# Windowed attention and an MLP mixer: 32-bit transposes of q and k pairs, natural order for the first two groups, and v loaded on 128 partitions

## Chip, cores and metric

The kernel runs on one core of one Trainium2 chip. The metric is the time of one execution on the device, in microseconds (us). A run that is more than 1.5% above the fastest of its kernel counts as slow and is left out of the ratios. Engine names: PE is TensorE (PEld its weight loads), DVE is VectorE, ACT is ScalarE, POOL is GpSimd, SP is SyncE. The program fixes the order of each engine's instructions, and in the traces one that waits holds up those behind it: after the change k of group 1 is cast at 41.85 us, right behind v's cast, and at 25.08 us when it is put ahead of it (run 1). In the DMA views q1 is SP's queue, q10 ACT's and q0 (software) POOL's.

## The reference

Four batches, eight heads, 768 positions, 64 columns per head; a window of 128 plus four sink positions. The attention output is the input x (768 x 512 per batch) of an MLP mixer.

```python
scores = scale * (q @ k.T);  keep = (pos_k < 4) | ((rel >= 0) & (rel < 128))
x = softmax(where(keep, scores, -1e9)) @ v            # (B, S, H*D)
u = x + (relu(x.T @ w_tok1) @ w_tok2).T               # token mixing, w_tok1 768x256, w_tok2 256x768
out = u + relu(u @ w_ch1) @ w_ch2                     # channel mixing, w_ch1 512x1536, w_ch2 1536x512
```

## The kernel before

The kernel handles eight groups of four heads, two groups per batch. Per group, q, k and v arrive as fp32, are cast to bf16, q and k are transposed in 32x32 blocks on DVE, scores run on 32-row tiles of PE, ACT takes the exps, DVE or POOL multiplies by masks, PE multiplies by v, and DVE normalises into x_b. When both groups of a batch are there, token mixing, u, the transposed u and then the channel mixer (ps_v with w_ch1, ps_w with w_ch2) follow.

The author's own planner fixes the order of the instructions of each engine. It simulates durations and landing times and picks, again and again, the operation that could start first.

```python
def order_of(ops, slots):
    ...
        if o.land:                                   # a DMA: modelled landing time
            dma_free = max(dma_free, t + 1.2) + o.land
            o.end = dma_free + 0.9
```

A dependency in this list orders the plan. It becomes a wait on the chip only where one instruction really reads or overwrites what the other one writes.

```python
    def load_ops(g, deps, pri):                      # cut
        run = E if g < 2 else 1                      # 1 KB runs for groups 0 and 1, 256 B later
        ...
                    e = "ACT" if g == 0 and w == "k" else "SP"
                        head_load(nc.scalar if e == "ACT" else nc.sync, G, w, heads(src, g), h, lo, hi, run)
    ...
        def turn(w, hf, db, c):                      # two 16-bit transposes for each of q and k
                nc.vector.transpose(G.T[w][:, db, ds(hf * HS, S // n_half)],
                                    G.bf[w][:, hf].rearrange("p (r x j) -> p r x j", x=DB, j=Q)[:, :, db])
    ...
    def weight(key, dst, src, deps, pri=-40):
        def emit(e):
            nc.gpsimd.dma_start(out=dst, in_=src)    # casts fp32 to bf16 on the way
    v1st = groups[0].load["v"][3]                    # "after v of group 0": known to the planner only
    weight("tok1", w_tok1, ..., [v1st]); weight("tok2", w_tok2, ..., [v1st])
    c1w = [weight(("ch1", i), ..., [v1st], ...) for i in range(4)]
```

For groups 0 and 1, v also comes in 1 KB runs of four rows, so it has to be spread to its rows by small matmuls (ps_p).

The softmax here doesn't subtract the row's maximum and nothing guards it: scores larger than these inputs give would overflow.

Of the kernel before, what the change touches and what calls it, by code (L numbers as in the profile page):

```python
# [12 lines left out]
ALU = mybir.AluOpType  # L13

# [10 lines left out]
class Op:  # L25


    n = 0

    def __init__(self, name, engines, emit, deps=(), pri=0, rows=False, take=(), free=(), land=0.0, dear=None):  # L30
        self.name, self.engines, self.emit = name, engines, emit
        self.deps, self.pri, self.rows = [d for d in deps if d is not None], pri, rows
        self.take, self.free, self.land, self.dear = take, free, land, dear or {}
        self.far = 0.0
        self.begin = self.end = self.engine = None
        Op.n += 1
        self.seq = Op.n
# [11 lines left out]
def order_of(ops, slots):  # L49
# [3 lines left out]
    dma_free, rows = 1.9, False  # L53
    for o in reversed(sorted(ops, key=lambda o: o.seq)):
        for d in o.deps:
            d.far = max(d.far, o.far + min(o.engines.values()) + (0.2 if "PE" in d.engines else 0.07))
# [3 lines left out]
    def start(op, e):  # L60
# [3 lines left out]
        if op.take:  # L64
            for kind in {p.kind for p in op.take}:
                n = sum(p.kind == kind for p in op.take)
                t = max(t, sorted(banks[kind])[n - 1])
        if e == "PE" and op.rows != rows:
            t += 0.095
        return t  # L70

    while waiting:
# [16 lines left out]
        t, e, o = best  # L89
        o.begin, o.engine = t, e  # L90
# [3 lines left out]
        if o.land:  # L94
            dma_free = max(dma_free, t + 1.2) + o.land
            o.end = dma_free + 0.9
        else:
# [22 lines left out]
def kernel(  # L120
# [101 lines left out]

    def c_ident(e):
        make_identity(nc, ident)
# [7 lines left out]
    def c_mneg(e):  # L232
        z = mneg.rearrange("p m (x c e i) -> p (m x) c e i", c=2, e=E, i=Q)
        nc.gpsimd.affine_select(out=z[:, :, 0], in_=z[:, :, 0], compare_op=ALU.is_ge, fill=-30000.0, base=0,
                                pattern=[[0, 4], [1, E], [E, Q]], channel_multiplier=-1)
        nc.gpsimd.affine_select(out=z[:, :, 1], in_=z[:, :, 1], compare_op=ALU.is_ge, fill=-30000.0, base=-1,
                                pattern=[[0, 4], [-1, E], [-E, Q]], channel_multiplier=1)
# [57 lines left out]
    BW, BWV = 0.37, 0.17  # L295
# [4 lines left out]
    def head_load(eng, G, w, src, h, lo, hi, run):  # L300

        n = (hi - lo) // (Q * run)
        at = lo // (Q * run)
        eng.dma_start(  # L304
            out=G.raw[w][Q * h:Q * h + Q].rearrange("p (c x) -> p c x", x=run * D)[:, at:at + n],
            in_=src[h, lo:hi].rearrange("(c i e) d -> i c (e d)", i=Q, e=run))

    def load_ops(g, deps, pri):
# [3 lines left out]
        run = E if g < 2 else 1  # L312
        for w, src in (("q", q), ("k", k), ("v", v)):
            if w == "v" and g >= 2:
                def vv(e):
                    t = G.raw["v"] = raw_tile("v")
                    nc.sync.dma_start(out=t.rearrange("p (h t d) -> p (h t) d", h=GH, t=NT),
                                      in_=heads(v, g).rearrange("h (t p) d -> p (h t) d", p=P))
                G.load["v"] = [op(f"Lv{g}", ("SP", 0.87), vv, deps, pri + 1, land=mb / BWV)]
                continue  # L320
            parts = [(0, HS), (HS, S)] if g == 0 and w != "v" else [(0, S)]
            G.load[w] = []
            for lo, hi in parts:
                for h in range(GH):
                    e = "ACT" if g == 0 and w == "k" else "SP"

                    def emit(_, w=w, src=src, h=h, lo=lo, hi=hi, e=e):
                        if w not in G.raw:
                            G.raw[w] = raw_tile(w)
                        head_load(nc.scalar if e == "ACT" else nc.sync, G, w, heads(src, g), h, lo, hi, run)  # L330
                    G.load[w].append(op(f"L{w}{g}.{lo}{h}", (e, 0.47), emit, deps,
                                        pri + (w == "v") * (50.5 if g == 0 else 1) + (lo > 0), land=mb / 4 * (hi - lo) / S / (BW if g < 2 else BWV)))


    def attention(g, xb, base):
# [3 lines left out]
        perm, pem = g < 2, g < 1  # L339
        early = base - 30 if perm else base  # L340
# [5 lines left out]
        def cast(w, hf):  # L346
# [5 lines left out]
            if perm:  # L352
# [3 lines left out]
            deps = G.load[w][4 * hf:4 * hf + 4] if first else G.load[w]  # L356
            return op(f"C{w}{g}.{hf}", eng, emit, deps + (prev.dt[w] if prev else []), early, dear={"DVE": 0.5 * g})

        def turn(w, hf, db, c):
            def emit(e):  # L360
                if w not in G.T:
                    G.T[w] = att.tile([P, DB, S], BF16, name=w + "T")
                nc.vector.transpose(G.T[w][:, db, ds(hf * HS, S // n_half)],  # L363
                                    G.bf[w][:, hf].rearrange("p (r x j) -> p r x j", x=DB, j=Q)[:, :, db])
            old = (prev.sc + [prev.sk]) if prev else []
            return op(f"T{w}{g}.{hf}{db}", ("DVE", dve(nc_ / 2) - 0.06), emit, [c] + old, early)

        casts, dts = {}, {"q": [], "k": []}
        for hf in range(n_half):
            for w in "qk":  # L370
                casts[w, hf] = cast(w, hf)
            for w in "qk":
                dts[w].append([turn(w, hf, db, casts[w, hf]) for db in range(DB)])
# [5 lines left out]
        if perm:  # L379
            def castv(e):  # L380
                G.vb = bfp.tile([P, NT, E, D], BF16, name="vb")
                copy_on[e](G.vb.rearrange("p t e d -> p (t e d)"), G.raw["v"])
            N = GH * S * D // P
            cv = op(f"Cv{g}", {"POOL": 1.02e-3 * N, "DVE": dve(N, 2)}, castv, G.load["v"], -5,
                    dear={"DVE": 0.3})
            ph = [Psum("mx", 1) for _ in range(GH)]

            G.cv = []
            for h in range(GH):
                def spread(e, h=h):  # L390
                    r = ds(Q * h, Q)
                    open_psum(ph[h], [P, NT, D], FP32, "ps_p")
                    for x in range(E):
                        nc.tensor.matmul(ph[h].tile[ds(Q * x, Q)], ident[r, r], G.vb[r, :, x],
                                         start=True, stop=True, tile_position=(Q * h, Q * x))
                sp = op(f"VP{g}.{h}", ("PE", 0.18), spread, [cv, c_ident_op], -5, rows=2, take=[ph[h]])

                def take(e, h=h):
                    copy_on[e](G.va[:, h, :, 0:D], ph[h].tile)
                G.cv.append(op(f"VE{g}.{h}", {"ACT": act(NT * D), "DVE": dve(NT * D)}, take, [sp, c_va_op] + old,  # L400
                               -5, free=[ph[h]]))
            G.cast.append(cv)
        else:
            def castv(e):
                copy_on[e](G.va[:, :, :, 0:D], G.raw["v"].rearrange("p (h t d) -> p h t d", h=GH, t=NT))
            G.cv = [op(f"Cv{g}", {"POOL": 1.55}, castv, G.load["v"] + [c_va_op] + old, base + 2)]
            G.cast += G.cv

        def sinkkeys(e):
            nc.vector.tensor_tensor(  # L410
                out=kz[g % 2][:, :, 0:4 * GH].rearrange("p x (h s) -> p x h s", h=GH),
                in0=(G.T["k"][:, :, 0:P:Q] if perm else G.T["k"][:, :, 0:4]).rearrange(
                    "p x (o s) -> p x o s", o=1).to_broadcast([P, DB, GH, 4]),
# [6 lines left out]
        def scores(u, hs, ps):  # L420
# [3 lines left out]
            def emit(e):  # L424
# [3 lines left out]
                if pem:  # L428
                    for h in hs:
                        nc.tensor.matmul(bank[h][:, 0:n], ident_e, mneg[:, min(u, 1), 0:n],  # L430
                                         start=True, stop=False, skip_group_check=True)
                at = 0
                for kt, w in nk:
                    for db in range(DB):
                        for h in hs:
                            r = ds(Q * h, Q)
                            nc.tensor.matmul(bank[h][:, at:at + w], G.T["k"][r, db, ts(kt, P)],  # L437
                                             G.T["q"][r, db, ds(kt * P, w)],
# [6 lines left out]
            if pem:  # L445
                dur += 0.19 + len(hs) * (n / 2400 + 0.003)
                deps += [c_mneg_op]
# [19 lines left out]
        def masks(u, ex):  # L467
# [21 lines left out]
            for x in xs:  # L489
                for c in range(2 if 2 * u + x < NT - 1 else 1):  # L490
                    r.append(op(f"MK{g}.{u}{x}{c}", {"DVE": dve(512, 2)} if perm else {"POOL": 0.72, "DVE": dve(512, 2) + 0.1}, lambda e, x=x, c=c: block(e, x, c),
# [21 lines left out]
        def sink_scores(e):  # L513
            ps = open_psum(pk_ps, [P, 512], FP32, "ps_k")
            for db in range(DB):
                nc.tensor.matmul(ps, kz[g % 2][:, db], G.T["q"][:, db, 2 * P:S], start=db == 0, stop=db == DB - 1)
# [53 lines left out]
    def mixer(b, base, mbase):  # L570
# [23 lines left out]
        M.t2, M.u, M.ut, M.ute = [], [], [], []  # L594
        M.ut_sb, M.u_sb = None, None
        M.uT = [None, None]
        cols = [(a, a * W, W) for a in range(GB)] if b == 0 else [(None, 0, DM)]
        M.ute = [[] for _ in range(NT)]
        for a, lo, n in cols:
            h1s = M.h1 if a is None else M.h1[NTOK * a:NTOK * a + NTOK]  # L600
            for st in range(NT):
                p, p2 = Psum("mx", 1), Psum("mx", 1)

                def tok2(e, st=st, p=p, lo=lo, n=n):
                    ps = open_psum(p, [P, n], FP32, "ps_u")
                    for tt in range(NTOK):
                        nc.tensor.matmul(ps, w_tok2[:, tt, ts(st, P)], M.h1t[:, tt, ds(lo, n)],  # L607
                                         start=(tt == 0), stop=(tt == NTOK - 1))

                def uadd(e, st=st, p=p, lo=lo, n=n):  # L610
# [201 lines left out]
```

## Time and profile before

| | before |
|---|---|
| time | 225.53 us (median of 2 runs, 225.16 to 225.91) |
| busy: PE, DVE, ACT, POOL | 206.2, 127.4, 107.5, 70.2 us |
| v of group 1 has landed (its cast starts) | 26.56 us |
| first channel-mixer matmul | 47.69 us |
| from there to the last PE work | 173.0 us |

These are the row of the page with busy times, and the row of the clock that TensorE was granted, in 40 slices of 5.6 us (9 is full speed).

```profile
PE 206.2 (92%) x1760; PEld 115.9 (52%) x1780; DVE 127.4 (57%) x271; ACT 107.5 (48%) x187; POOL 70.2 (31%) x89
...
PEclk9955569999999999999999999999999999999999
```

The next view is the table of windows: start:end, length, then busy time and instructions of each engine, the granted clock, the share of the DMA engines and GB/s.

```profile
core 0: us, PE busy (x) PEld busy (x) DVE busy (x) ACT busy (x) POOL busy (x), PEclk, DMA share, GB/s
0.00:12.00 12.00, 6.74 (x27) 2.42 (x28) 8.33 (x18) 3.51 (x6) 7.35 (x22) 0.98 0.97 174
12.00:32.00 20.00, 15.98 (x139) 6.70 (x139) 12.16 (x23) 9.99 (x16) 9.03 (x12) 0.50 1.24 199
...
48.00:221.00 173.00, 169.97 (x1433) 96.88 (x1449) 93.16 (x187) 86.31 (x150) 52.33 (x54) 1.00 0.65 116
```

From 48 us on PE is busy for 169.97 of 173 us, so that stretch is bound by PE. Everything before it is a start-up of 48 us that waits for data. The chain of waits (start, duration, what), read around that start-up, shows for what:

```profile
10.88 7.93 DMA raw_k<-in_k_dram
18.82 7.61 DMA raw_v<-in_v_dram
26.56 1.36 DVE vb L199
27.96 1.43 PE ps_p L394 x12
...
47.69 2.38 PE ps_v L645 x14
```

The DMA view from 20 to 26 us (queue, packets, MB, share of 16 engines' time) has one line of data, SP's queue; no weight packet moved before about 26 us, when v of group 1 was in:

```profile
q1 hardware_dynamic: 1907, 1.21, 117.9%
```

Of the groups of instructions these lines concern the change: transposes and masks (count, busy us, mean ns).

```profile
L212 POOL TENSOR_SCALAR_AFFINE_SELECT pT<-pT 128x512 bf16<-128x512 bf16 x21 | 15.9, 765 | 35.4 <-ACT pT L456 14.9
...
L363 DVE STREAM_TRANSPOSE kT<-kb 128x768 bf16<-128x768 bf16 (+1 forms) x18 | 15.0, 863 | 11.4 <-POOL kb L200 10.7
```

### The profile page before, as it was taken

The numbers are of one execution on the slowest core, as the hardware profiler recorded it, in microseconds if no ns is written. First come the engines' busy times: TensorE is split into PE (matmuls) and PEld (weight loads), VectorE is DVE, ScalarE is ACT, GpSimd is POOL, SyncE is SP. The second block draws the span as 40 slices with busy tenths as digits, with TensorE's granted clock in tenths as the row PEclk, the third lists the DMA queues.
The fourth block names the chain that finished last, engine by engine and source line by source line (L and its number), as shares of the span: only waits on it lengthen the run. The fifth ranks groups of instructions, "written<-read, shape, count | busy, mean of one in ns | idle before, by whom it ended". The sixth has DMA issues, their size and how long they took to land.

```text
span 223.9 us, 4412 instructions
## 1 busy us (share of the span) xinstructions
PE 206.2 (92%) x1760; PEld 115.9 (52%) x1780; DVE 127.4 (57%) x271; ACT 107.5 (48%) x187; POOL 70.2 (31%) x89
## 2 busy tenths in 40 slices
PE   7298497999999999999999899999999999999994
PEld 2023165766557546555656554456755544655543
DVE  7665498780378558958948984698672113001122
ACT  0466346357574481489583470288653400763300
POOL 6616800200467265418639232174200000000000
PEclk9955569999999999999999999999999999999999
DMA  7999999999999199899999499500001112101122
GB/s 149 200 202 207 186 194 192 193 197 199 180 164 209 39 198 171 210 195 169 190 167 202 114 166 189 194 3 3 0 1 40 56 47 94 50 0 47 47 97 94
DMA packets 70212, 29.40 MB, mean 131 GB/s; under 512 B 57776, under 2 KB 67248, under 8 KB 70192
## 3 DMA queue, kind: packets, MB, share of 16 engines
q1 hardware_dynamic: 63984, 24.39, 61.8%
q0 software_dynamic: 5312, 3.95, 11.6%
q10 hardware_dynamic: 896, 0.79, 1.8%
q8 instruction: 14, 0.23, 0.5%
q14 instruction: 6, 0.05, 0.1%
HBM read 26.77 MB, written 6.29 MB: 148 GB/s over the span
## 4 chain that ended last, share of the span: by engine, by line
PE 75%; DMA 10%; DVE 7%; ACT 4%; SPq 1%; issue 1%; DVEq 0%
PE ps_w L667 27%; PE ps_v L645 26%; DMA raw_k<-in_k_dram 7%; PE ps_u L607 5%; PE ps_h L583 5%; PE ps_s L437 4%; DMA raw_v<-in_v_dram 3%; PE ps_ut L618 3%; DVE pT L477 2%; PE ps_o L538 2%; PE ps_o L543 2%; PE ps_o L535 2%; DVE x_b L559 2%; ACT pT L456 1%; SPq L304 1%
## 5 line engine op out<-in xcount | busy, mean ns | idle before, releaser
L645 PE MATMUL ps_v<-uT,w_ch 128*128 128x384 bf16 x384 | 69.0, 326 | 0.8 <-DVE x_b L559 0.6
L667 PE MATMUL ps_w<-w_ch,v 128*128 128x512 bf16 (+1 forms) x288 | 65.2, 370 | 0.8 <-issue 0.2
L205 ACT ACTIVATE v<-ps_v 128x384 bf16<-128x384 f32 x86 | 42.0, 493 | 43.2 <-PE ps_v L645 32.1
L645 PEld LDWEIGHTS <-w_ch 128*128 128x128 bf16 x384 | 35.8, 98 | 24.8 <-DVE x_b L559 1.7
L677 DVE TENSOR_TENSOR o<-ps_w,u_sb 128x512 f32<-128x512 f32 (+1 forms) x25 | 16.7, 666 | 52.0 <-PE ps_w L667 52.0
L667 PEld LDWEIGHTS <-v 128*128 128x128 bf16 x300 | 28.6, 98 | 30.2 <-issue 0.4
L456 ACT ACTIVATE pT<-ps_s 128x1024 bf16<-128x1024 f32 (+1 forms) x36 | 32.4, 950 | 20.2 <-PE ps_s L437 17.7
L212 POOL TENSOR_SCALAR_AFFINE_SELECT pT<-pT 128x512 bf16<-128x512 bf16 x21 | 15.9, 765 | 35.4 <-ACT pT L456 14.9
L437 PE MATMUL ps_s<-qT,kT 32*128 32x256 bf16 (+1 forms) x384 | 20.0, 281 | 2.6 <-DVE kT L363 1.9
L363 DVE STREAM_TRANSPOSE kT<-kb 128x768 bf16<-128x768 bf16 (+1 forms) x18 | 15.0, 863 | 11.4 <-POOL kb L200 10.7
L559 DVE TENSOR_TENSOR x_b<-ps_o,rc 128x256 bf16<-128x256 f32 x48 | 20.4, 424 | 1.6
L200 POOL CAST kb<-raw_k 128x1536 bf16<-128x1536 f32 x7 | 10.4, 1491 | 26.8 <-DMA raw_k<-in_k_dram 26.8
L437 PEld LDWEIGHTS <-kT 32*128 32x128 bf16 x384 | 10.2, 97 | 16.0 <-issue 10.7
L613 DVE TENSOR_TENSOR u_sb<-ps_u,x_b 128x512 bf16<-128x512 f32 (+1 forms) x30 | 15.6, 573 | 4.2 <-PE ps_u L607 4.2
L538 PE MATMUL ps_o<-va,pT 128*128 128x65 bf16 x192 | 16.8, 199 | 0.1
L538 PEld LDWEIGHTS <-pT 128*128 128x128 bf16 x192 | 14.5, 101 | 2.6 <-issue 0.7
L543 PE MATMUL ps_o<-va,pT 128*128 128x65 bf16 x160 | 15.6, 198 | 0.0
L363 DVE STREAM_TRANSPOSE qT<-qb 128x768 bf16<-128x768 bf16 (+1 forms) x18 | 15.0, 865 | 0.2 <-POOL qb L200 0.2
L607 PE MATMUL ps_u<-h,w_tok 128*128 128x512 bf16 (+1 forms) x57 | 13.3, 333 | 0.9 <-ACT h L205 0.6
L200 POOL CAST qb<-raw_q 128x1536 bf16<-128x1536 f32 x6 | 9.0, 1494 | 13.1 <-DMA raw_q<-in_q_dram 12.5
L201 ACT ACTIVATE uT<-ps_ut 128x512 bf16<-128x512 bf16 (+1 forms) x17 | 8.4, 509 | 9.0 <-PE ps_ut L618 8.7
L477 DVE TENSOR_TENSOR pT<-pT,mrest 128x512 bf16<-128x512 bf16 x17 | 11.8, 715 | 1.0 <-ACT pT L456 0.9
(74 smaller groups left out, 193.5 us busy)
## 6 DMA issues: line engine op xcount, KB each, us to landing
out_dram<-o SPq DMA_DIRECT2D x23, 256.0 KB, 2.1
raw_q<-in_q_dram SPq DMA_DIRECT2D x28, 192.0 KB, 5.8
raw_k<-in_k_dram SPq DMA_DIRECT2D x28, 192.0 KB, 6.5
raw_v<-in_v_dram SPq DMA_DIRECT2D x6, 768.0 KB, 8.2
raw_v<-in_v_dram SPq DMA_DIRECT2D x8, 192.0 KB, 7.6
w_ch<-in_moe_w_ch_dram POOLq DMA_DIRECT2D x4, 384.0 KB, 16.8
w_ch<-in_moe_w_ch_dram POOLq DMA_DIRECT2D x1, 1024.0 KB, 25.6
raw_q<-in_q_dram SPq DMA_DIRECT2D x8, 96.0 KB, 3.7
```

The source lines that it names most:

```text
L200: "POOL": lambda o, i: nc.gpsimd.tensor_copy(out=o, in_=i),
L205: nc.scalar.activation(o, i, AF.Relu)
L363: nc.vector.transpose(G.T[w][:, db, ds(hf * HS, S // n_half)], G.bf[w][:, hf].rearrange("p (r x j) -> p r x j", x=DB, j=Q)[:, :, db])
L437: nc.tensor.matmul(bank[h][:, at:at + w], G.T["k"][r, db, ts(kt, P)], G.T["q"][r, db, ds(kt * P, w)], start=not pem and db == 0, stop=db = ...
L456: nc.scalar.activation(o, i, AF.Exp, scale=scale)
L538: nc.tensor.matmul(ps[:, h], G.pT[qt // 2][:, h, ds(256 * (qt % 2), P)], G.va[:, h, qt], start=(qt < 2 and h == 0), stop=(h == GH - 1 and ...
L543: nc.tensor.matmul(ps[:, h], G.pT[kt // 2][:, h, ds(256 * (kt % 2) + P, P)], G.va[:, h, kt], start=False, stop=(h == GH - 1), skip_group_c ...
L559: nc.vector.tensor_tensor(out=xb.tile[:, qt, c0:c0 + W].rearrange("p (h d) -> p h d", h=GH), in0=ps[:, :, 0:D], in1=rc.to_broadcast([P, GH ...
L607: nc.tensor.matmul(ps, w_tok2[:, tt, ts(st, P)], M.h1t[:, tt, ds(lo, n)], start=(tt == 0), stop=(tt == NTOK - 1))
L645: nc.tensor.matmul(ps, w_ch1[:, c, ts(ft, P)], M.uT[hf][:, c], start=(c == 0), stop=(c == NC - 1))
L667: nc.tensor.matmul(p.tile, M.v1t[hf][:, ft, ts(st % NH, P)], w_ch2[:, ft, ds(lo, n)], start=(ft == 0), stop=(ft == NF - 1))
L677: nc.vector.tensor_tensor(out=box["o"], in0=p.tile, in1=M.u_sb[:, st, ds(lo, n)], op=ALU.add)
```

## The change

The intent is a shorter start-up and less work on DVE and POOL. (1) Two neighbouring bf16 values are moved as one 32-bit element, so one transpose replaces two. (2) For groups 0 and 1 the transposes write with 16-byte steps, which brings q and k into natural order; v of these groups is loaded straight onto 128 partitions, in runs of 256 bytes, and the spread on PE falls away. (3) All q and k come in 1 KB runs. Heads 2 and 3 are issued by ACT for groups 0 and 1 and by POOL after that. (4) Groups 2 to 7 become the permuted ones (their positions stay in the order that the 1 KB runs of four rows bring, and their masks are reordered to match), and these masks run on DVE alone. (5) Batch 0 forms the transposed u directly by matmuls and its ordinary u later. (6) In the plan, token weights follow k of group 0 and channel weights follow v of group 1. (7) The planner fills PE's gaps before 36 us with dummy matmuls.

```diff
-        run = E if g < 2 else 1
+        near, far_ = (nc.sync, "SP"), (nc.scalar, "ACT") if g < 2 else (nc.gpsimd, "POOL")
+        for w, src in (("q", q), ("k", k)):
+            G.load[w] = [issue(w, f"L{w}{g}.{h}", near if h < 2 else far_, GH * S * D * 1e-6 / BW, ...)
+                         for h in range(GH)]
+        if g in NAT:                                  # groups 0 and 1
+            def vv(eng):
+                eng.dma_start(out=G.raw["v"].rearrange("p (n d) -> p n d", d=D),
+                              in_=heads(v, g).rearrange("h (t p) d -> p (h t) d", p=P))
...                                                    # 32-bit transposes, one per tensor
-            cv = op(f"Cv{g}", {"POOL": 1.02e-3 * N, "DVE": dve(N, 2)}, castv, G.load["v"], -5,
+        veng = {"POOL": 1.02e-3 * N}
+        if g < 2:
+            veng |= {"DVE": dve(N, 2), "ACT": act(N)}
...
+        direct = b == 0                               # ps_ut = h.T w_tok2 + x.T, by matmul
...
-    weight("tok1", w_tok1, ..., [v1st])
-    weight("tok2", w_tok2, ..., [v1st])
+    weight("tok1", w_tok1, ..., [groups[0].load["k"][3]], -40, 60)
+    weight("tok2", w_tok2, ..., [groups[0].load["v"][0]], -40, 135)
     c1w = [weight(("ch1", i), ...,
-                  [v1st], [-40, 12, 14, 16][i]) for i in range(4)]
+                  [groups[1].load["v"][0]], -40 + i, 78) for i in range(4)]
...
+    class Filler:
+        until = 36.0
```

## The prediction

> **What bounds the kernel.** Two stretches. From 47.7 us on, TensorE is full: in the chain of waits the channel-mixer matmuls start at 47.69 us (line 645) and TensorE work then runs to 220.7 us. Counting that work at the durations of the chain (a tile of four 128x384 matmuls 0.65 us, twelve 128x512 matmuls 2.6 us, scores 0.55/0.55/0.44 us per step, sinks 0.54 us) gives about 168 us of the 173, so only some 5 us of gaps are left there. Before 47.7 us the kernel waits: the chain is DMA of k, then v, until 26.5 us (the 40-slice row shows about 200 GB/s), then the v spread, second group's scores, exps and masks, token mixing, u and its transposes. The same stretch has TensorE at clock 0.5 from about 12 to 31 us (window table). Useful TensorE work there is only some 17 us, an estimate from the same durations at full clock.
>
> **What the change does.**
> 1. Head loads go on two queues, heads 0,1 on one and 2,3 on the other.[...] I expect 260 to 350 GB/s for q and k; v in 256-byte runs near 190 to 225.
> 2. Warm-up matmuls fill TensorE's startup gaps, so the clock should stay at 1.0.
> 3. The v spread (0.55 and 1.43 us chains on TensorE plus copies) goes.
> 4. q, k: one 32-bit transpose replaces two 16-bit ones (956 ns each for 768 columns): about 0.9 us less per tensor. The 16-byte-step ones of the first two groups may be slower per element.
> 5. Batch 0 forms u transposed by matmul: the stretch from the last token-mixing h (about 42.9 us) to 47.7 us shrinks to about 1.5 us, but about 2 us of transposed tiles and 2.6 us of ordinary u tiles (6 x 0.43) now come after the channel mixer begins: +4.6 us of TensorE work.
> 6. Groups 2 to 7 become permuted: 37 POOL masks of 765 ns go to VectorE, where they take about 420 ns uncontended; that cancels most of its transpose saving. ScalarE exps of the last step split in two (2 x 502 for 808 ns).
> 7. Weights of token mixing load earlier and compete with group 1.
>
> **Critical path.** Steady state is TensorE-bound; 4 and 6 are worth -2 to +1 us. The gain is the earlier channel mixer start. Estimate: q0, k0 land near 7.5 us, v0 11 to 13, q1, k1 17 to 20, v1 21 to 24; second group's attention done near 31; first channel-mixer matmul at 34 us (range 30 to 40). That is 13.7 us earlier, minus 4.6 us added, and about 1 us less of gaps: 225.5 - 10 = 215.5 us.
>
> **Prediction:** 215.5 us, 208 to 222 in 8 of 10. Faster by over 2%: 0.82, within: 0.15, slower: 0.03.
>
> **What would show it.** Clock 1.0 in slices 3 to 6; GB/s above 260 in the first slices; line of the channel mixer first in the chain near 34 us; its end minus start still about 176 to 178 us; POOL busy down from 70 to about 45 us; transposes halved in count, about 0.9 us each; VectorE about unchanged.
>
> **What would make it wrong.** [...]16-byte-step transposes taking twice as long; second-layer weights landing late and stalling the mixer; POOL-issued loads waiting behind POOL's casts so that groups 2, 3 come late; masks on VectorE delaying token mixing.

The author's estimate: 260 to 350 GB/s for q and k, and the landing times that rest on it. For comparison, the trace before shows 206 GB/s from 12 to 20 us, nearly all on SP's queue (83 ns a packet: 113.1% of 16 x 8 us over 1744), and 187 GB/s from 25 to 26 us, where 696 of 709 packets are under 512 B. The sum itself: 225.5 less 13.7, plus 4.6, less about 1 is 215.4, which the prediction rounds to 225.5 - 10 = 215.5 us; but its 13.7 rests on those landings. That the dummy matmuls would hold the clock at 1.0 was an estimate too: in the trace before it is 0.50 from 12 to 20 us, where PE is busy for all of 8.00 us, and 1.00 from 48 to 221 us.

## More of the kernel before

One more view turned out to matter more than I saw when I predicted. It is the timeline of POOL (start, duration, instruction, in brackets the idle time before it and what ended that).

```profile
18.96 1.46 POOL L200 CAST kb<-raw_k 128x1536 bf16<-128x1536 f32 x1 [3.55 <-DMA raw_k<-in_k_dram]
20.37 1.59 POOL L735 DMA_DIRECT2D w_tok<-in_moe_w_tok_dram  x2
21.94 5.18 POOL L735 DMA_DIRECT2D w_ch<-in_moe_w_ch_dram  x6
```

The weights are issued at 20.37 us because the instruction before them, the cast of group 1's k, had to wait for its data; no weight packet moved before about 26 us, when v of group 1 was in. A cast stands like a gate in front of the weights.

## The result and the profile after

The time after is 243.51 us (median of 2 runs, 243.09 to 243.94), against 225.53 us. The ratio is 1.0797, with a 95% interval of 1.0686 to 1.0908. A ratio here is always the mean time of one kernel's fast runs over that of the other's of the same rounds, so it is not quite the ratio of the medians that are quoted. The change makes the kernel 8% slower; the prediction had it 4% faster.

| us | before | after |
|---|---|---|
| weights of the channel mixer are issued | 21.94 | 17.10 |
| v of group 1 landed (cast starts) | 26.56 | 40.98 |
| first channel-mixer matmul | 47.69 | 60.91 |
| from there to the last PE work | 173.0 | 177.9 |

The first matmul of the mixer comes 13.2 us later and the rest is 4.9 us longer. Together that is 18.1 of the 18.3 us by which the profiled spans differ (223.9 and 242.2 us).

The same two rows of the page after:

```profile
PE 214.6 (89%) x1780; PEld 121.1 (50%) x1800; DVE 123.0 (51%) x275; ACT 104.9 (43%) x188; POOL 59.9 (25%) x81
...
PEclk9997995559999999999999999999999999999999
```

Windows of the kernel after, with the columns as before:

```profile
0.00:20.00 20.00, 16.90 (x126) 7.70 (x127) 11.45 (x20) 8.42 (x10) 13.91 (x31) 1.00 1.10 216
...
32.00:43.00 11.00, 0.00 (x0) 0.00 (x0) 1.99 (x3) 0.10 (x1) 0.00 (x0) 0.65 1.21 211
...
61.00:239.00 178.00, 173.17 (x1450) 98.54 (x1463) 96.29 (x221) 84.98 (x159) 33.94 (x36) 1.00 0.46 97
```

Between 32 and 43 us PE runs nothing at all, although the DMA engines are busy throughout (share 1.21, 211 GB/s). The timeline of DVE says what it waits for:

```profile
19.16 0.98 DVE L215 CAST qb<-raw_q 128x1536 bf16<-128x1536 f32 x1 [2.14 <-DMA raw_q<-in_q_dram]
...
40.98 0.96 DVE L215 CAST va<-raw_v 128x1536 bf16<-128x1536 f32 x1 [16.06 <-DMA raw_v<-in_v_dram]
41.85 0.95 DVE L215 CAST kb<-raw_k 128x1536 bf16<-128x1536 f32 x1
42.84 1.53 DVE L387 STREAM_TRANSPOSE kT<-kb 128x768 uint32<-128x768 uint32 x1
```

and the timeline of PE, where it goes on:

```profile
44.43 1.06 PE L440 MATMUL ps_s<-qT,kT 32*128 32x256 bf16 x16 [12.64 <-DVE kT L387]
...
60.91 1.30 PE L670 MATMUL ps_v<-uT,w_ch 128*128 128x384 bf16 x7
```

DVE stands 16.06 us in front of the cast of group 1's v. The cast and the transpose of group 1's k stand behind it in DVE's fixed order. That v was issued on SP at 16.49 us (timeline of SP), so it took 24 us; until about 22 us SP's queue still moved mostly k of group 1, in 1 KB packets (127 packets with 0.11 MB from 21 to 22 us, 179 with 0.05 MB from 22 to 23):

```profile
16.49 0.39 SPq L344 DMA_DIRECT2D raw_v<-in_v_dram  x1
```

POOL's timeline after shows that the weights no longer wait for anything of group 1, because the planner gave the cast of k to DVE:

```profile
17.10 4.99 POOL L763 DMA_DIRECT2D w_ch<-in_moe_w_ch_dram  x6
```

The DMA view between 28 and 40 us splits what moved by queue (packets, MB, share of 16 engines' time). Weights are q0; q1 is v, with a few packets of the next group's q and k.

```profile
q0 software_dynamic: 2014, 1.79, 90.2%
q1 hardware_dynamic: 2017, 0.57, 33.3%
```

The two queues move the same **number** of packets, 2014 and 2017, but three times as many bytes go to the weights. v's packets are 256 bytes, the weights' 768 or 1024 (889 on average, 1.79 MB over 2014). An average weight packet took 86 ns of an engine (90.2% of 16 x 12 us, over 2014), one of q1 32 ns. At this rate, 2017 packets in 12 us, the 3072 packets of v take an estimated 18 us, which fits 22 to 40 us.

The trace of the kernel before held the same pattern, and I overlooked it before predicting. There q and k of group 2 come in 256-byte packets beside the weights, from 28 to 40 us:

```profile
q0 software_dynamic: 2308, 1.79, 96.7%
q1 hardware_dynamic: 1909, 0.48, 30.4%
```

From 32 us on the counts are 1515 and 1514. It cost little there: PE was busy for 169.97 of the 173 us from 48 us on.

What makes the counts equal, and how many packets one queue gets before the other has its turn, the traces do not show.

The groups of DVE after, split by form:

```profile
L480 DVE TENSOR_TENSOR pT<-pT,mrest_e 128x512 bf16<-128x512 bf16 x54 | 20.7, 436 | 0.3 <-ACT pT L465 0.2
L387 DVE STREAM_TRANSPOSE qT<-qb 128x768 uint32<-128x768 uint32 x7 | 7.4, 1051 | 4.5 <-POOL qb L216 4.5
```

### The profile page after: what moved, and what is told of

Its sections match the earlier page's. It is cut to its first block, busy times and chain, and to the rows that moved or that the text cites. A ratio compares the mean times of both kernels' runs of the same rounds, so it can differ in the third digit from the quotient of the medians.

```text
span 242.2 us, 4426 instructions
## 1 busy us (share of the span) xinstructions
PE 214.6 (89%) x1780; PEld 121.1 (50%) x1800; DVE 123.0 (51%) x275; ACT 104.9 (43%) x188; POOL 59.9 (25%) x81
## 5 line engine op out<-in xcount | busy, mean ns | idle before, releaser
L221 ACT ACTIVATE v<-ps_v 128x384 bf16<-128x384 f32 x84 | 41.0, 494 | 43.9 <-PE ps_v L670 32.1
L461 ACT ACTIVATE pT<-ps_s 128x1024 bf16<-128x1024 f32 x24 | 23.4, 1021 | 17.8 <-PE ps_s L440 17.0
L440 PE MATMUL ps_s<-qT,kT 32*128 32x256 bf16 (+1 forms) x384 | 18.9, 279 | 13.2 <-DVE kT L387 12.6
L642 DVE TENSOR_TENSOR u_sb<-ps_u,x_b 128x512 bf16<-128x512 f32 x24 | 15.0, 680 | 13.1 <-PE ps_v L670 9.2
L480 DVE TENSOR_TENSOR pT<-pT,mrest_e 128x512 bf16<-128x512 bf16 x54 | 20.7, 436 | 0.3 <-ACT pT L465 0.2
L804 PE MATMUL ps_warm<-warm 128*128 128x512 bf16 x59 | 16.9, 447 | 1.8 <-DVE warm L237 1.3
L459 ACT ACTIVATE pT<-ps_s 128x1024 bf16<-128x1024 f32 (+1 forms) x12 | 11.2, 952 | 16.2 <-PE ps_s L440 15.9
L216 POOL CAST qb<-raw_q 128x1536 bf16<-128x1536 f32 x6 | 8.8, 1467 | 35.5 <-DVE x_b L562 13.6
L541 PEld LDWEIGHTS <-pT 128*128 128x128 bf16 x192 | 14.6, 101 | 2.8 <-issue 1.0
L538 PE MATMUL ps_o<-vsink,pk 128*128 128x260 bf16 x32 | 9.3, 292 | 4.3 <-DVE x_b L562 4.2
L546 PEld LDWEIGHTS <-pT 128*128 128x128 bf16 x160 | 12.2, 103 | 0.6
L586 PE MATMUL ps_h<-x_b,w_tok 128*128 128x256 bf16 x96 | 12.1, 273 | 0.4 <-DVE x_b L562 0.3
## 6 DMA issues: line engine op xcount, KB each, us to landing
raw_v<-in_v_dram SPq DMA_DIRECT2D x2, 768.0 KB, 18.1
```

Source lines behind the costliest of these rows:

```text
L221: nc.scalar.activation(o, i, AF.Relu)
L440: nc.tensor.matmul(bank[h][:, at:at + w], G.T["k"][r, ts(kt, P), db], G.T["q"][r, ds(kt * P, w), db], start=not pem and db == 0, stop=db = ...
L461: nc.scalar.activation(o.rearrange("p h (x i e) -> p (h x) i e", i=Q, e=E), i.rearrange("p h (x e i) -> p (h x) i e", i=Q, e=E), AF.Exp, s ...
L480: nc.vector.tensor_tensor(out=t, in0=t, op=ALU.mult, in1=(mrest_e if perm else mrest)[:, ts(c, P)].rearrange("p (o x) -> p o x", o=1).to_b ...
L541: nc.tensor.matmul(ps[:, h], G.pT[qt // 2][:, h, ds(256 * (qt % 2), P)], G.va[:, h, qt], start=(qt < 2 and h == 0), stop=(h == GH - 1 and ...
L546: nc.tensor.matmul(ps[:, h], G.pT[kt // 2][:, h, ds(256 * (kt % 2) + P, P)], G.va[:, h, kt], start=False, stop=(h == GH - 1), skip_group_c ...
```

## The experiments

Theory A: v of group 1 arrives late because its small packets run beside the weights' large ones, which POOL now issues early. Rival B: the order on DVE, where v's cast stands ahead of k's, costs the time, and v's landing matters little. Theory C in the first texts: the new transposes or a lower clock cost it. Runs 1 to 4, 5 to 8, 9 to 12, 13 to 16, and 17 and 18 ran each on one chip and shared their runs of the kernel before. Run 10 has no ratio and is told of below.

| run | edit on | median us | ratio to before, 95% | v of group 1 cast | mixer starts |
|---|---|---|---|---|---|
| 1 k first | after | 240.98 | 1.0688 (1.0646 to 1.0730) | 41.03 | 57.42 |
| 2 gate | after | 238.18 | 1.0540 (1.0496 to 1.0584) | 28.54 | 45.37 |
| 3 v in 1 KB | after | 232.50 | 1.0311 (1.0242 to 1.0381) | 29.39 | 47.32 |
| 4 gate, k first | after | 238.36 | 1.0581 (1.0535 to 1.0627) | 28.54 | 47.46 |
| 5 gate, SP loads | after | 232.47 | 1.0331 (1.0287 to 1.0374) | 28.30 | 47.34 |
| 6 and not direct | after | 228.85 | 1.0154 (1.0110 to 1.0197) | 27.98 | 48.80 |
| 7 pairs alone | before | 227.26 | 1.0074 (1.0053 to 1.0096) | 27.17 | 50.95 |
| 8 v in 256 B | before | 225.09 | 0.9980 (0.9943 to 1.0017) | 25.57 | 46.52 |
| 9 all gated | after | 236.94 | 1.0487 (1.0426 to 1.0547) | 25.10 (landed 24.1) | 52.60 |
| 11 and slower plan | after | 235.15 | 1.0389 (1.0297 to 1.0481) | 27.32 (landed 25.7) | 50.44 |
| 12 v in 256 B, weights early | before | 238.75 | 1.0585 (1.0506 to 1.0665) | 42.22 | 61.05 |
| 13 run 6, slower plan | after | 230.59 | 1.0217 (1.0179 to 1.0255) | no profile | no profile |
| 14 fillers | before | 226.25 | 1.0031 (0.9999 to 1.0064) | 26.57 | 48.01 |
| 15 split by ACT | before | 229.20 | 1.0176 (1.0136 to 1.0215) | 22.88 | 53.13 |
| 16 fillers, split, slower plan | before | 235.07 | 1.0397 (1.0347 to 1.0448) | 34.42 (slow run) | 55.62 (slow run) |
| 17 split by ACT and POOL | before | 231.15 | 1.0238 (1.0189 to 1.0287) | 27.23 or 29.44 | 52.21 |
| 18 and slower plan | before | 224.63 | 0.9955 (0.9915 to 0.9996) | between 23.20 and 24.4 | 48.65 |

### Runs 1 to 4: starved v, or the order on DVE?

**Run 1.** k of group 1 is cast and transposed ahead of v.

```diff
-        G.cv = [op(f"Cv{g}", veng, castv, G.load["v"] + [c_va_op] + old, ...
+        G.cv = [op(f"Cv{g}", veng, castv, G.load["v"] + [c_va_op] + old + (G.dt["k"] if g == 1 else []), ...
```

> Only VectorE's order changes: the cast and the transpose of the second group's k stand ahead of the cast of its v. Theory A (the second group's v, 256-byte packets, starves beside the weights' packets and lands at 41 us; the order only makes it worse): v still lands near 41 us, the scores of the second group start near 26 us instead of 44.4, the channel mixer starts near 49 us instead of 60.9, time about 231 to 233 us. Theory B (the in-order queue of VectorE is the whole cause, v's landing is no limit): channel mixer near 36 us, about 218 us. Theory C (32-bit and 16-byte-step transposes or a lower clock are the cause): no change, 242 to 244 us.

Measured: 240.98 us. These two lines are from the timelines of DVE and PE of this run.

```profile
41.03 0.96 DVE L215 CAST va<-raw_v 128x1536 bf16<-128x1536 f32 x1 [13.42 <-DMA raw_v<-in_v_dram]
```

```profile
42.14 1.03 PE L519 MATMUL ps_k<-qT,kz 128*128 128x512 bf16 x2 [7.70 <-DVE kz L413]
```

k's transpose now ran at 26.06 us, but v landed as late as before, and the next DVE work stood behind it. The order is worth about 2.5 us (243.51 to 240.98). That is not the main part, against B, and against C, which expected no change. A's own numbers for this run (mixer near 49 us, 231 to 233 us) were missed too: kz, the sink keys, still stood behind v's cast on DVE, as the second line shows, so the run tests B only in part.

**Run 2.** One column of v is copied on POOL ahead of the channel weights. This is a real data dependency: POOL can issue these weights only when v has landed.

```diff
+    gate_t = singles.tile([P, 1], FP32, name="gate")
+    def c_gate(e):
+        nc.gpsimd.tensor_copy(out=gate_t, in_=groups[1].raw["v"][:, 0:1])
+    o_gate = op("gate", ("POOL", 0.1), c_gate, [groups[1].load["v"][0]], -41)
-                  [groups[1].load["v"][0]], -40 + i, 78) for i in range(4)]
+                  [o_gate], -40 + i, 78) for i in range(4)]
```

> A one-column POOL copy that reads the second group's v stands before the channel-mixer weights' DMA issues, so these really wait until v has landed. Theory A: v lands at about 21 to 23 us instead of 41, channel mixer starts at 36 to 39 us, time 217 to 221 us, faster than before (225.5). Theory B: v lands earlier and VectorE's queue no longer holds k up, so the same direction; told apart by e1 and e4. Theory C: channel mixer stays above 50 us.

Measured: v's cast began at 28.54 us instead of 40.98, and the mixer at 45.37, 15.5 us earlier. C, with the mixer above 50 us, is out. But v, mixer and time all missed what A expected, and the time fell only by 5.3 us. The rest was lost in a new hole, shown by the window from 55 to 60 us and by POOL's timeline.

```profile
55.00:60.00 5.00, 0.07 (x2) 0.01 (x1) 1.62 (x3) 0.00 (x0) 3.12 (x3) 0.96 0.31 63
```

```profile
28.57 0.97 POOL L772 COPY gate<-raw_v 128x1 f32<-128x1 f32 x1 [11.73 <-DMA raw_v<-in_v_dram]
29.49 5.06 POOL L763 DMA_DIRECT2D w_ch<-in_moe_w_ch_dram  x6
...
56.88 1.46 POOL L216 CAST qb<-raw_q 128x1536 bf16<-128x1536 f32 x1 [15.00 <-issue]
```

PE stood still because POOL's cast of q of group 2 came only after 15 us of idling. Half of that q is issued on POOL's own queue, behind the channel weights. The trace names no releaser ("issue"); that this queue is what POOL waits for is tested in run 5. This second cost had been hidden in the kernel after, where the first one was larger.

**Run 3.** v of group 1 is loaded in 1 KB packets as before, without the spread, so the result is wrong (relative error 0.43). The mechanism that A's packet form named is cut from the text below as not shown; what is left of it is the equal counts of the kernel after (2014 and 2017 packets), with which the size of the packets sets the share of the bytes.

```diff
             def vv(eng):
+                if g == 1:
+                    for h in range(GH):
+                        head_load(eng, G, "v", heads(v, g), h)
+                    return
```

> Result wrong on purpose: the second group's v is loaded with 1 KB packets by four 32-partition DMAs, in a layout that the kernel doesn't want; nothing else changes, the weights still compete. Theory A in its packet form[...]: v lands at 26 to 29 us, channel mixer at 41 to 45 us, 223 to 227 us. If the queue's place or the bytes alone set the share, v lands near 41 us as before and the time stays near 243 us.

Measured: 232.50 us, v's cast at 29.39. The weights are as early as in the kernel after; only v's packets are larger. The DMA view of this run, from 28 to 40 us:

```profile
q0 software_dynamic: 1894, 1.59, 81.5%
q1 hardware_dynamic: 1892, 1.03, 40.7%
```

The counts are equal again, and the bytes of q1 nearly double (1.03 for 0.57 MB). So bytes follow packet size here. This one edit brings the mixer's start back by 13.6 us (47.32 for 60.91) and the time by 11.0 us, though mixer and time stay above the expected ranges.

**Run 4.** Both edits of runs 1 and 2.

> Both e1 and e2. Theory A: once v lands before or with k the order is worth under 1 us, so within 1 us of e2. Theory B: clearly faster than e2.

Measured: 238.36 us, the same as run 2 within its interval. With v on time, the order on DVE is worth nothing (the mixer even starts 2 us later). A stands for the stall; B explains the 2.5 us of run 1. How much more it would explain with kz, too, ahead of the late v was not run.

### Runs 5 to 8: what else the change costs

**Run 5.** Run 2, and SP issues heads 2 and 3 of groups 2 to 7.

```diff
-  (nc.scalar, "ACT") if g < 2 else (nc.gpsimd, "POOL")
+  (nc.scalar, "ACT") if g < 2 else (nc.sync, "SP")
```

> e2 with one more edit: from the third group on, the loads of heads 2 and 3 are issued by SP and no longer by POOL. In e2 POOL waited 15 us for the third group's q, TensorE then sat still from 55 to 60 us, and the work from the first channel-mixer matmul to the last matmul took 188 us instead of 178. Theory A (those loads stand behind 6.3 MB of channel weights in POOL's own DMA queue): q lands 8 us or more before it is needed, the stall at 55 us goes, first to last matmul 177 to 180 us, time 226 to 229 us. Rival (DMA bandwidth as a whole is short there, whoever issues): the stall stays and the time stays near 238 us.

Measured: 232.47 us. First to last matmul of the bound stretch took 179.7 us, as expected. The hole is gone, as the same window shows:

```profile
55.00:60.00 5.00, 4.73 (x35) 2.04 (x34) 4.18 (x7) 2.54 (x5) 1.47 (x1) 1.00 1.21 226
```

The time missed the expected range by 3.5 us. Of this 2 us are the mixer's later start than in run 2 (the plan changed with the edit); the rest I did not trace.

**Run 6.** Run 5 with ordinary u for batch 0 (`direct = False`).

> e5 with batch 0's u formed and transposed as in the kernel before, not directly. The direct form takes 8 transposed tiles and delays 6 ordinary ones past the start of the channel mixer (4.6 us of TensorE work), and by the trace saves some 2.5 us ahead of it. Theory: channel mixer starts 2 to 3 us later than in e5, first to last matmul 4 to 5 us shorter, time 1 to 3 us lower than e5. Rival (the direct form pays for itself): e6 not lower than e5.

Measured: 228.85 us, 3.6 us less than run 5. The mixer starts 1.5 us later, but from there to the end it takes 175.4 instead of 179.7 us. The direct form costs PE more in the bound stretch than it saves ahead of it.

**Run 7.** The kernel before with 32-bit pairs alone.

```diff
-                    G.T[w] = att.tile([P, DB, S], BF16, name=w + "T")
-                nc.vector.transpose(G.T[w][:, db, ds(hf * HS, S // n_half)], ...[:, :, db])
+                    G.T[w] = att.tile([P, S, 2], BF16, name=w + "T")
+                o = G.T[w].rearrange("p s x -> p (s x)")[:, ds(hf * nc_, nc_)].bitcast(UINT32)
+                nc.vector.transpose(o, G.bf[w][:, hf].bitcast(UINT32))
```

> The kernel before with the 32-bit pairs alone: each q and k transposed by one 32-bit instruction of 768 columns instead of two 16-bit ones, TensorE reads q and k with a 4-byte step. Theory: VectorE's 36 transposes become 18 of about 0.95 us, 12 us less VectorE work; TensorE is full after 47.7 us and reads the step at the same speed, so the time changes by less than 1%, 223 to 225.5 us. Rival (the 4-byte step slows TensorE): scores take more than 0.55 us per step and the time rises by more than 1%.

Measured: DVE's busy time falls from 127.4 to 116.0 us, and the kernel is 0.7% slower, not faster. DVE bounds neither stretch. A slowing of PE by the 4-byte step hardly shows: the sixteen-matmul steps of the scores took 0.63, 0.64 and 0.52 us from 61 to 68 us, against 0.61, 0.61 and 0.51 from 59 to 67 us in the kernel before. The shorter durations also let the planner choose another order, and the mixer started at 50.95 us; that the order is the cause is likely, but I did not isolate it. The plan moved the cast of group 1's k to DVE here, so POOL issued the weights as early as in the kernel after, and v in its 1 KB packets still came only 0.6 us later than before:

```profile
17.39 5.02 POOL L736 DMA_DIRECT2D w_ch<-in_moe_w_ch_dram  x6
```

```profile
27.17 0.96 DVE L200 CAST vb<-raw_v 128x1536 bf16<-128x1536 f32 x1 [3.84 <-DMA raw_v<-in_v_dram]
```

**Run 8.** The kernel before with v of groups 0 and 1 in 256-byte packets (wrong, relative error 0.60, since the spread remains).

```diff
+                        if w == "v":
+                            if h == 0:
+                                nc.sync.dma_start(out=G.raw[w].rearrange("p (n d) -> p n d", d=D),
+                                                  in_=heads(v, g).rearrange("h (t p) d -> p (h t) d", p=P))
+                            return
```

> Result wrong on purpose: the kernel before, in which v of the first two groups comes by one 128-partition DMA each with 256-byte packets (values then in the wrong places; all else stays). Theory A: the second group's v, beside the weights' packets, lands at 36 to 43 us instead of 26.5, and the kernel before becomes as slow as the changed one, 234 to 241 us. If 128 partitions make up for the packet size, v lands by 27 us and the time stays within 2 us of 225.5.

Measured: 225.09 us, no loss at all. This was a miss for A as I had stated it. The DMA view of this run from 20 to 24 us has one single line of data:

```profile
q1 hardware_dynamic: 3418, 0.87, 134.8%
```

The first weights were issued at 19.98 us, but no packet of theirs moved before 24 us. SP's queue had the engines to itself and moved its 256-byte packets at 218 GB/s. Why the weights' packets came so late, no run here shows. So small packets alone cost nothing here. A now needs both halves: small packets **and** large packets of another queue at the same time. Run 12 tests that.

### Runs 9 to 12: both halves of the cause, and what is left

**Run 9.** Run 6, k first, and the token weights behind the gate too.

> e6 with two more edits: k's cast and transpose ahead of v's on VectorE (as in e1), and the token-mixing weights too wait until the second group's v has landed. In e2 those 1.57 MB still ran beside the first loads and v landed at 28.5 us. Theory (what is left of the loss is DMA time taken by weights): v lands at 22 to 25 us, channel mixer starts at 43 to 46 us instead of 48.8, time 223 to 227 us. Rival (what is left is TensorE's fixed order with warm-up matmuls and the first group's token mixing ahead of the second group's scores): v lands earlier but the mixer starts within 2 us of e6, time 227 to 230 us.

Measured: 236.94 us, a miss by much for theory and rival. v landed early (24.1 us), but PE's timeline shows what was traded for it:

```profile
34.07 1.46 PE L586 MATMUL ps_h<-x_b,w_tok 128*128 128x256 bf16 x6 [6.38 <-DMA w_tok<-in_moe_w_tok_dram]
```

Token mixing of group 0 stands ahead of most of group 1 in PE's fixed order, and waited 6.4 us for weights that now came too late.

**Run 10.** Run 9 with fillers only up to 9 us (`until = 9.0`).

> e9 with the warm-up matmuls only up to 9 us of the planned order, not to 36. In e4 11 of them ran at 28.2 to 30.8 us and 8 at 38.4 to 41.5 us, where the real waits were elsewhere. Theory (they stand in the way): mixer starts 2 to 4 us earlier than in e9. Rival (they keep the clock up and cost nothing): the clock falls to 0.5 in part of 20 to 40 us and the mixer starts later, time higher than e9 by 1 us or more.

Measured: four runs from 234.72 to 241.45 us, of which only one counts as fast. The profiled run is that fast one (234.72 us): its mixer began at 48.51 us, 4.1 us before run 9's, about as the theory had it, and the clock fell to 5 tenths in two slices, as the rival had it (mean over the span 0.963, run 9's 0.978). One run is a hint that the fillers stood in the way there, no more.

**Run 11.** Run 9 with slower loads in the plan (`BW = 0.25`, and 0.19 in place of 0.225 for v), closer to the measured landings.

> e9 with the DMA rates of the kernel's own planner set to what the traces show (0.25 instead of 0.35 for q and k, 0.19 instead of 0.225 for v), so that its fixed order plans with later landings. Theory (the planned order, made for data that come earlier than they do, costs the rest): mixer starts 2 us or more earlier than in e9, time below before (under 224 us). Rival: within 1 us of e9.

Measured: 235.15 us, 1.8 us below run 9 but still far from before, and 11 us above what the theory expected; a plan with better landing times doesn't cure this order.

**Run 12.** Run 8 with the weights early: the casts of group 1's k and of both v's are kept off POOL, and the weights follow k of group 0 in the plan. This takes the accidental gate of the kernel before away.

```diff
             if perm:
                 eng |= {"DVE": dve(nc_, 2)}
+            if g == 1 and w == "k":
+                del eng["POOL"]
...
-            cv = op(f"Cv{g}", {"POOL": 1.02e-3 * N, "DVE": dve(N, 2)}, castv, ...
+            cv = op(f"Cv{g}", {"DVE": dve(N, 2)}, castv, ...
...
-    v1st = groups[0].load["v"][3]
+    v1st = groups[0].load["k"][7]
```

> Result wrong on purpose: e8 (the kernel before, v of the first two groups in 256-byte packets, which cost nothing there) with the casts of the second group's k and of the first v taken off POOL, so that POOL no longer waits for that k before it issues the weights. E8 missed because in the kernel before POOL stood still until k had landed (18.6 us) and the weights' data began at about 24 us, when v was nearly in. Theory A, as corrected (small packets cost only where the weights' packets run at the same time): weights are issued at about 15 us, v of the second group lands at 33 to 43 us, time 231 to 241 us. If small packets are harmless even then, 225 to 228 us.

Measured: 238.75 us. One line of DVE's timeline, then two of the DMA view from 28 to 40 us:

```profile
42.22 0.96 DVE L199 CAST vb<-raw_v 128x1536 bf16<-128x1536 f32 x1 [14.60 <-DMA raw_v<-in_v_dram]
```

```profile
q0 software_dynamic: 2139, 1.76, 90.9%
q1 hardware_dynamic: 2137, 0.55, 34.2%
```

The stall of the kernel after is rebuilt inside the kernel before, with its equal counts, its start of the mixer (61.05 for 60.91) and most of its time, inside the range that A expected. The square of the two factors is complete; it gives when v's cast of group 1 began:

| | channel weights early | channel weights late |
|---|---|---|
| v in 256-byte packets | 40.98 (after), 42.22 (run 12) | 28.54 (run 2), 25.57 (run 8) |
| v in 1 KB packets | 29.39 (run 3), 27.17 (run 7) | 26.56 (before) |

Runs 7, 8 and 12 and the kernel before make the same square within one kernel: 256-byte packets beside early weights cost about 16 us, either one alone no more than 0.6.

### Runs 13 to 18: can any part of the change be kept?

Still open was why the start-up gains nothing even where v comes on time. These runs take one part each.

**Run 13.** Run 6 with the slower plan of run 11.

> e6 with the planner's DMA rates set to the measured ones (0.25 for q and k, 0.19 for v, sum with the token weights 27.9 us, measured 28). Theory (TensorE's fixed order, planned for data 5 us earlier than they come, puts the first group's token mixing and warm-up matmuls ahead of the second group's scores): mixer starts 2 us or more before e6's 48.8, time 224 to 227 us. Rival (the chain of exps, masks and value products after v has this length anyway): within 1 us of e6.

Measured: 230.59 us, no better than run 6, so the theory missed. One of its runs, the profiled one, took 765 us; it is left out, and there is no usable profile.

**Run 14.** The kernel before with the fillers in place of its 14 dummy matmuls.

> The kernel before with the planner's warm-up matmuls up to 36 us, nothing else. The clock row should read 9 or more where it read 5 from 11 to 31 us. Theory: the waits there are DMA and ScalarE, TensorE at half clock costs only the value products and scores after v has landed, so channel mixer 1 to 3 us earlier and 222.5 to 225 us. Rival (clock is not on the chain): within 0.5 us of before.

Measured: 226.25 us, the same as before, as the rival had it. The clock rows are 9998558999 here and 9955569999 before, in the first ten slices (mean over the span 0.970 in the profiled run, 0.946 to 0.953 in the runs of the kernel before). So the fillers didn't keep the clock up to the end of the start-up, but half clock shrank from three slices to two, and that was worth nothing where PE waits for data.

**Run 15.** The kernel before with heads 2 and 3 of groups 0 and 1 issued by ACT.

```diff
-  e = "ACT" if g == 0 and w == "k" else "SP"
+  e = "ACT" if g < 2 and h >= 2 else "SP"
```

> The kernel before with the loads of heads 2 and 3 of the first two groups (q, k and v, 1 KB packets) on the ScalarE queue and those of heads 0 and 1 on SP, nothing else. Theory[...]: the first 10 us show 260 to 300 GB/s instead of 200 and 1 KB packets of about 60 ns instead of 82 to 91, v of the second group lands at 19 to 22 us instead of 26.5, channel mixer 2 to 5 us earlier, 220 to 224 us. Rival[...]: v at 25 us or later, time within 1 us of before.

Measured: 229.20 us. The DMA engines did deliver more: 2.09 MB in the first 10 us, against 1.82 MB in run 14, and a packet of q1 and q10 took 48 ns on average (70.0% of 16 x 10 us over 2326), against 70 (88.6% over 2038). But ACT had to issue the loads itself and stood in that work; its first own instruction is this line of its timeline:

```profile
17.27 1.28 ACT L201 ACT_TABLE_LOAD   x1 [17.27 <-DMA raw_v<-in_v_dram]
```

v's cast began at 22.88 us, 3.7 us earlier than before, yet the mixer began 5.4 us later. The exps began only at 19.11 us. Theory and rival both missed the time.

**Run 16.** Fillers, the split of run 15, and 0.25 in the plan for the first two groups' rate.

> e14 and e15 together, with the planner's rate for these loads at 0.25. Theory: the two gains add, 218 to 223 us, faster than both kernels. Rival: no better than the better of the two.

Measured: 235.07 us, far from the expected 218 to 223; the profiled run was a slow one, so I read no mechanism from it beyond ACT's late start (17.13 us), as in run 15.

**Run 17.** ACT issues heads 2 and 3 only of group 0's q and k; POOL issues those of group 1 and of v.

```diff
-  e = "ACT" if g == 0 and w == "k" else "SP"
+  e = ("ACT" if g == 0 and w != "v" else "POOL") if g < 2 and h >= 2 else "SP"
```

> The kernel before with heads 2 and 3 of the first two groups on a second queue: ScalarE issues only those of the first group's q and k (8 issues, as many as in the kernel before), POOL those of the second group and of v. Theory: ScalarE is free by 8 us, v of the second group lands at 21 to 24 us instead of 26.5, mixer starts 2 to 5 us earlier, 220.5 to 224 us, faster than both kernels. Rival (an earlier v gives the time back elsewhere, in the order planned for other landings): within 1 us of before.

Measured: 231.15 us, a miss for both. POOL came to group 1's loads only from 15.1 to 19.1 us, since it waited for the sinks of v first, and the casts of the two v began at 27.23 and 29.44 us.

**Run 18.** Run 17 with 0.25 in the plan.

> e17 with the planner's rate for these loads at 0.25 instead of 0.37. Theory: closer to the measured landings, 0 to 2 us below e17. Rival: within 0.5 us of e17 or above it.

Measured: 224.63 us (224.21 to 226.33), ratio 0.9955 (0.9915 to 0.9996). It is the only version with right results whose ratio lies below 1, by less than half a per cent, and no win by the measure of 2%. The casts of both v ran from 23.20 to 25.35 us, so both were done before the second one began in the kernel before (26.56 us); the mixer still started 1 us later, at 48.65 us, in the profiled run, which with 226.33 us was the slowest of the six.

## Why the prediction was wrong

**The step that failed.** The prediction said "q1, k1 17 to 20, v1 21 to 24; second group's attention done near 31; first channel-mixer matmul at 34 us". Measured were 40.98 us for v1 and 60.91 us for the mixer. This term alone, 26.9 us, is nearly all of the miss of 28.0 us. It has two parts, worked out with 22.5 us as the middle of the predicted landing:

- v landed 18.5 us later than predicted. Shown: the 256-byte packets of v ran beside the weights' packets, and the queues took equal numbers of packets (after, runs 3 and 12). I had asked how fast two queues are, not who shares the engines. I did list that the weights of token mixing "compete with group 1", but gave it no cost, and overlooked that POOL would come to the channel weights at 17.10 us. The dependency on v that the diff gives to these weights is only the planner's; I took it for a wait.
- From v's landing to the mixer took 19.9 us, where I had assumed 11.5 (34 less 22.5). The kernel before needs 21.1 (47.69 less 26.56), which its profile showed. Runs 2 to 6 brought v to between 27.98 and 29.39 us, and the mixer still began between 45 and 49 us. Part of that length is the fixed order of PE, where other work stands ahead of group 1 (run 9 shows one such wait). In no run was it under 16.4 us (run 1), so what it takes to reach 11.5 stays open.

**First landings.** q and k of group 0 came nearly as predicted (casts at 5.99 and 9.18 us, for 7.5), q of group 1 too (19.16 us, for 17 to 20). k of group 1 did not: its packets still moved at 21 to 22 us, for 17 to 20. v of group 0 came at 16.06 us, not at 11 to 13.

**Two queues.** The rate of the two queues, an estimate, was not what failed. Predicted were 260 to 350 GB/s for q and k; from 2 to 8 us the kernel after moved 277 GB/s, the kernel before 219. Both have two queues busy then; before, ACT carries k beside SP's q, in DMAs of 96 KB, and after, each queue carries its own heads of both, in DMAs of 192 KB, so the rise is not shown to come from the split alone. These are the DMA views from 0 to 9 us, before and then after:

```profile
DMA packets 1781, 1.55 MB, mean 172 GB/s; under 512 B 272, under 2 KB 1781, under 8 KB 1781
```

```profile
DMA packets 2262, 1.87 MB, mean 208 GB/s; under 512 B 534, under 2 KB 2262, under 8 KB 2262
```

Run 15, which changes the queues alone, moved 15% more bytes than run 14, which changes the fillers alone, in the first 10 us (2.09 for 1.82 MB; it compares two whole kernels, so the figure is rough). The gain was lost again in the engines that issue (runs 15 and 17).

**Fillers.** Predicted to keep the clock at 1.0. It was 1.00 up to 20 us, 0.69 from 20 to 24, 0.93 from 24 to 36, and it fell to 0.50 from 36 to 54, in the stall and behind it. Run 14, with half clock in fewer slices, was no faster; a start-up at full clock throughout was not run. What sets the clock no run here isolates, and it was not what made v late: runs 2 and 3 keep the fillers, and v's cast began at 28.54 and 29.39 us.

**Direct transposed u.** Predicted at +4.6 us of PE work against a lead-in that shrinks from 4.8 to 1.5 us. Right: the bound stretch took 177.9 us, inside the predicted 176 to 178, and from the last ps_h matmul to the mixer it is 2.3 us after for 5.2 before. But by these figures of its own the prediction had this part as a loss of 1.3 us, and I did not draw that conclusion. Without this form the kernel is 3.6 us faster (run 6 against 5).

**Transposes and masks.** Right. DVE is about unchanged, 123.0 for 127.4 us. The masks on DVE took 436 ns on average, for the predicted 420 "uncontended", which is what the trace before shows: 420 on average for nine of them (mrest_e), one of 0.41 us at 150.11 us with POOL all but idle, and one of 1.40 us at 148.24 us, beside POOL's cast of v at 147.90 us. The count of transposes halved and one of q takes 1051 ns on average, most of them about 0.97 us and the ones with 16-byte steps 1.53 us. So with contiguous output 768 elements of 32 bits cost about what 768 of 16 bits did before (956 ns). POOL fell to 59.9 us, not to 45, since it now issues loads, which take it 13.7 us.

**What would make it wrong.** The list named loads of POOL that come late. They do, behind the weights rather than behind casts, but it shows only once the first cause is cured (run 2: about 6 us to run 5). It did not name v.

So the loss has these parts. The starved v with what hangs on it accounts for the later start of 13.2 us: run 3, which changes only v's packets, takes 13.6 us of it away. The order on DVE is 3.5 us of this start while v is late (run 1). The direct form accounts for most of the 4.9 us after that (the stretch is 4.3 us shorter in run 6 than in run 5). With v on time, the loads off POOL's queue and no direct form (run 6), the kernel is still 1.5% slower than before; its mixer starts 1.1 us later and the rest takes 2.4 us longer, and no run isolates why.

## What to carry to other kernels

Two DMA queues that were busy together took equal numbers of packets here (2014 and 2017 from 28 to 40 us), not of bytes (1.79 and 0.57 MB), and a critical load in 256-byte packets beside a bulk load in larger ones came about 16 us later (runs 7, 8, 12 and the kernel before). Where a trace shows such a pair, give the bulk load a real wait, a copy that reads the critical data (run 2: v's cast at 28.54 for 40.98 us); a dependency in this planner was none. Before moving an operation to another engine, ask what stands behind it in the old engine's stream: the cast of k on POOL had held the weights back, and nobody had written that down. And look for the sharing in the old trace first: it was there, on group 2's q and k. In this start-up, bound by data, a clock at half in two slices for three (run 14, 226.25 us) and a DVE less busy by 11.4 us (run 7, 227.26 us) were worth nothing; cost the chain behind the last load from the old trace, not from the sum of its durations.
